# Score matmuls of a head pair as two 64-row array tiles, with the PSUM banks divided 5, 1, 2 instead of 3, 2, 3

## The chip, the cores and the metric

The kernel runs on one core of one Trainium2 chip. The metric is the device time of the kernel in microseconds (us), measured on that core. "Clock" is the share of full speed that the throttle granted TensorE. A profile is of one execution; its "span" is some 2 us shorter than the time.

## The reference

Eight batches of causal attention (by blocks of 64), eight heads of 64, sequence 576, followed by a token-mixing and a channel-mixing layer on the concatenated heads. Cut to what matters:

```python
# q, k, v: [8, 8, 576, 64] fp32, normal x 0.1
scores = q @ k.T / 8;  mask: 64-row block of the query >= 64-row block of the key
x  = softmax(scores) @ v                     # -> [8, 576, 512], heads side by side
h  = relu(x.T @ w_tok1) @ w_tok2             # token mix: 576 -> 256 -> 576
u  = x + h.T
out = u + relu(u @ w_ch1) @ w_ch2            # channel mix: 512 -> 1536 -> 512
```

## The kernel before

All matmuls are in bf16. The MLP of one batch runs between the attention of the next, and a scheduler orders the instructions of each engine. Per batch there are four head pairs. Q and K of a pair are transposed together, so head 0 lies in partitions 0 to 63 and head 1 in 64 to 127. The eight PSUM banks are divided among three pools, and every tile below takes one bank.

```python
ps_at = tile_pool("ps_at", bufs=3, PSUM)   # scores; probabilities times V also go here
ps_tr = tile_pool("ps_tr", bufs=2, PSUM)   # transposes of q, k and u
ps_mm = tile_pool("ps_mm", bufs=3, PSUM)   # MLP matmuls
...
# attention_pair: K of one head, the other head's 64 rows being zero (set at the start)
nc.vector.tensor_copy(kTh[0][0:64, :], kT_ps[0:64, :])        # L194
nc.scalar.copy(kTh[1][64:128, :], kT_ps[64:128, :])           # L195
for hh in range(2):
    kT = kTh[hh]
    sc = [ps_at.tile([128, 512], FP32, name="sc") for _ in range(4)]
    for J, (tix, c0, ist, wdt) in REGIONS.items():            # L214: 6 matmuls, 1600 columns
        nc.tensor.matmul(out=sc[tix][:, c0:c0+wdt], lhsT=kT[:, j0:j0+128],
                         rhs=qT[:, ist:ist+wdt], ...)         # 128 rows, 64 of them zero
    nc.scalar.activation(e[0], sc[0], EXP, scale=scale)       # L223 .. L226: 3 large, 1 small
    ...
    # L238: 15 matmuls of 65 columns into sc[3]; then normalised into x_sb
...
# transpose_u: for each of 5 row blocks: 4 transposes into ONE ps_tr bank (L301),
#              then nc.any.tensor_copy out of it (L306, mostly ScalarE)
# channel_gT:  24 groups of 4 matmuls of 288 columns into a ps_mm bank (L319),
#              each followed by a ReLU out of it (L326)
```

The softmax here doesn't subtract the row's maximum and nothing guards it: scores larger than these inputs give would overflow.

## Time and profile before

| | before |
|---|---|
| time, median of 2 runs | 415.43 us (415.31 to 415.54) |
| span of the profile | 412.9 us |
| TensorE recorded busy | 89% |
| ScalarE busy | 54% |
| one batch in the steady state | 46.2 us |

The waits of TensorE in the kernel before; the columns are engine, tile and line that waited, the releaser, then total us, number of waits, longest us.

```profile
PE sc L214 <- ACT e L223: 2.9, 15, 0.3
...
PE trp L301 <- ACT uT L306: 0.8, 2, 0.6
```

Scores and transposes wait for ScalarE for 3.7 us in the whole run. This is TensorE's timeline around one head pair of the kernel before (start us, length us, line, operation, count; in brackets idle time just before and its releaser):

```profile
222.89 0.82 PE L214 MATMUL sc<-qT,kTa 128*128 128x512 bf16 x5
223.55 0.59 PE L336 MATMUL mps<-wc_sb,gT 128*128 128x512 bf16 x2
224.22 0.19 PE L214 MATMUL sc<-qT,kTa 128*128 128x64 bf16 x1
224.25 0.59 PE L336 MATMUL mps<-wc_sb,gT 128*128 128x512 bf16 x2
224.71 0.38 PE L214 MATMUL sc<-qT,kTb 128*128 128x512 bf16 x1
```

Between the score matmuls (L214) stand matmuls of the second channel layer (L336).

### The profile page before, as it was taken

To read this page: it belongs to the slowest core of one execution; us is meant where nothing else is said; L and a number is where in the kernel's file an instruction comes from. 1 tells how busy PE (TensorE), PEld (TensorE's weight loads), DVE (VectorE), ACT (ScalarE), POOL (GpSimd) and SP (SyncE) were. 2 spreads that over 40 slices of the span, in tenths; PEclk is the share of its full clock that TensorE was granted. 3 is DMA by queue.
4 is the path that set the end of the run, shared out by engine and by line. 5 is a ranking of instruction groups with operands and counts; after the bars stand their busy time and mean duration, and the time that the engine had idled before them with its cause. 6 is when DMAs were issued, how large, how long until landed. Compare 5 with 4: busy or idle time off the path is not lost.

```text
span 412.9 us, 8622 instructions
## 1 busy us (share of the span) xinstructions
PE 368.6 (89%) x3194; PEld 229.3 (56%) x3232; DVE 175.8 (43%) x674; ACT 221.4 (54%) x507; POOL 261.0 (63%) x403
## 2 busy tenths in 40 slices
PE   1676659999999999999999999999999999999996
PEld 1454247754676456744666457744666457744752
DVE  2244324543545364543554363543555363534112
ACT  9635037742677058742687058732687068730830
POOL 9999389999999775983679375973679320000000
PEclk9998859999999999999999999999999999999999
DMA  6999999999988894785668494885658550003003
GB/s 40 103 60 111 206 78 58 59 60 152 74 58 57 52 156 31 51 54 128 42 41 54 33 154 30 52 52 129 44 38 51 51 110 0 2 2 114 2 2 114
DMA packets 124730, 27.91 MB, mean 68 GB/s; under 512 B 117200, under 2 KB 119568, under 8 KB 124688
## 3 DMA queue, kind: packets, MB, share of 16 engines
q0 software_dynamic: 119824, 17.92, 60.2%
q1 hardware_dynamic: 4864, 9.44, 6.3%
q8 instruction: 26, 0.43, 0.4%
q14 instruction: 16, 0.13, 0.1%
HBM read 35.78 MB, written 9.44 MB: 110 GB/s over the span
## 4 chain that ended last, share of the span: by engine, by line
PE 52%; ACT 22%; POOL 9%; DVE 8%; DMA 5%; issue 3%; ACTq 0%; POOLq 0%
PE mps L336 22%; PE mps L319 18%; ACT e L224 6%; ACT e L223 5%; ACT kTb L195 5%; DMA wc_sb<-in_moe_w_ch_dram 4%; PE sc L238 4%; ACT e L225 3%; PE sc L214 3%; DVE u_sb L290 3%; POOL qraw L116 2%; POOL v L202 2%; ACT uT L306 2%; DVE qT L188 1%; ACT gT L326 1%
## 5 line engine op out<-in xcount | busy, mean ns | idle before, releaser
L319 PE MATMUL mps<-uT,wc_sb 128*128 128x288 bf16 x768 | 111.6, 286 | 1.0
L336 PE MATMUL mps<-wc_sb,gT 128*128 128x512 bf16 x464 | 110.8, 379 | 0.8
L319 PEld LDWEIGHTS <-wc_sb 128*128 128x128 bf16 x768 | 71.0, 97 | 28.4 <-issue 10.6
L116 POOL DMA_DIRECT2D qraw<-in_q_dram x64 | 55.3, 864 | 43.8 <-PE trp L192 28.8
L326 ACT ACTIVATE gT<-mps 128x288 bf16<-128x288 f32 x144 | 59.0, 410 | 28.1 <-PE mps L319 20.7
L336 PEld LDWEIGHTS <-gT 128*128 128x128 bf16 x480 | 44.5, 98 | 50.8 <-issue 5.1
L195 ACT COPY kTb<-trp 64x640 bf16<-64x640 bf16 x32 | 22.0, 687 | 89.5 <-DVE kTa L194 89.1
L202 POOL DMA_DIRECT2D v<-in_v_dram x64 | 56.3, 880 | 21.4 <-PE sc L214 18.5
L116 POOL DMA_DIRECT2D kraw<-in_k_dram x64 | 56.5, 883 | 7.0 <-PE trp L192 5.2
L343 DVE TENSOR_TENSOR o_sb<-mps,u_sb 128x512 f32<-128x512 f32 (+1 forms) x40 | 27.6, 690 | 71.3 <-PE mps L336 71.3
L238 PEld LDWEIGHTS <-e 128*128 128x128 bf16 x960 | 41.6, 101 | 16.9 <-issue 6.9
L214 PE MATMUL sc<-qT,kTb 128*128 128x64 bf16 (+4 forms) x190 | 43.7, 292 | 2.9 <-issue 0.4
L122 POOL DMA_DIRECT2D kraw<-in_k_dram x64 | 42.3, 660 | 1.0 <-DMA wc_sb<-in_moe_w_ch_dram 1.0
L122 POOL DMA_DIRECT2D qraw<-in_q_dram x64 | 40.9, 640 | 2.7 <-DMA wc_sb<-in_moe_w_ch_dram 2.7
L238 PE MATMUL sc<-v,e 128*128 128x65 bf16 x900 | 41.7, 195 | 1.1 <-ACT e L226 0.8
L206 POOL DMA_DIRECT2D v<-in_v_dram x64 | 41.4, 647 | 0.4 <-PE sc L214 0.3
L225 ACT ACTIVATE e<-sc 128x512 bf16<-128x512 f32 x60 | 36.0, 600 | 3.3 <-PE sc L214 1.5
L224 ACT ACTIVATE e<-sc 128x512 bf16<-128x512 f32 x60 | 35.7, 595 | 3.7 <-PE sc L214 3.7
L223 ACT ACTIVATE e<-sc 128x512 bf16<-128x512 f32 x60 | 35.8, 597 | 3.4 <-PE mps L238 1.9
L306 ACT COPY uT<-trp 128x512 bf16<-128x512 bf16 (+1 forms) x36 | 19.5, 544 | 29.9 <-PE trp L301 28.8
L326 DVE TENSOR_SCALAR gT<-mps 128x288 bf16<-128x288 f32 x48 | 22.0, 458 | 26.1 <-PE mps L319 25.6
L214 PE MATMUL sc<-qT,kTa 128*128 128x64 bf16 (+4 forms) x162 | 27.8, 280 | 4.3 <-ACT e L223 2.6
(61 smaller groups left out, 367.9 us busy)
## 6 DMA issues: line engine op xcount, KB each, us to landing
out_dram<-o_sb SPq DMA_DIRECT2D x8, 1024.0 KB, 4.3
qraw<-in_q_dram POOLq DMA_DIRECT2D x64, 64.0 KB, 2.8
kraw<-in_k_dram POOLq DMA_DIRECT2D x64, 64.0 KB, 2.7
v<-in_v_dram POOLq DMA_DIRECT2D x64, 64.0 KB, 2.8
wc_sb<-in_moe_w_ch_dram POOLq DMA_DIRECT2D x4, 384.0 KB, 6.8
wc_sb<-in_moe_w_ch_dram POOLq DMA_DIRECT2D x6, 256.0 KB, 11.9
qraw<-in_q_dram POOLq DMA_DIRECT2D x64, 8.0 KB, 2.3
kraw<-in_k_dram POOLq DMA_DIRECT2D x64, 8.0 KB, 2.3
```

The costliest lines, as they stand in the source:

```text
L116: nc.gpsimd.dma_start(out=t[:, c0:c1, hh, :], in_=src[b, 2 * hp + hh, 128 * c0 : 128 * c1, :].rearrange("(c p) d -> p c d", p=128),)
L122: nc.gpsimd.dma_start(out=t[0:64, 4, hh, :], in_=src[b, 2 * hp + hh, 512:576, :])
L195: nc.scalar.copy(kTh[1][64:128, :], kT_ps[64:128, :])
L202: nc.gpsimd.dma_start(out=v1[:, 0:4, 0:64], in_=v[b, h, 0:512, :].rearrange("(c p) d -> p c d", p=128),)
L214: nc.tensor.matmul(out=sc[tix][:, c0 : c0 + wdt], lhsT=kT[:, j0 : j0 + 128], rhs=qT[:, ist : ist + wdt], start=True, stop=True,)
L223: nc.scalar.activation(e[0], sc[0], EXP, scale=scale)
L224: nc.scalar.activation(e[1][:, 0:512], sc[1], EXP, scale=scale)
L225: nc.scalar.activation(e[2][:, 0:512], sc[2], EXP, scale=scale)
L238: nc.tensor.matmul(out=u_view[:, I, 0:65], lhsT=exp_lhsT(e, I, J), rhs=v1[:, J, 0:65], start=(J == 0), stop=(J == I),)
L319: nc.tensor.matmul(out=g_ps[:, 0:288], lhsT=wc1_sb[:, m, 128 * cc : 128 * (cc + 1)], rhs=uT[:, m, 288 * sh : 288 * (sh + 1)], start=(m == ...
L326: nc.any.tensor_scalar_max(gT[:, cc, 288 * sh : 288 * (sh + 1)], g_ps[:, 0:288], 0.0)
L336: nc.tensor.matmul(out=h2_ps, lhsT=gT[:, cc, 128 * si : 128 * (si + 1)], rhs=wc2_sb[:, cc, :], start=(cc == 0), stop=(cc == NDC - 1),)
```

## The change

The intent: a score matmul contracts over 64 rows, and before it used all 128 rows of the array with zeros in half of them. Two matmuls on the two halves of the array can run side by side, so the 3200 columns of a head pair would take the time of 1600; K need not be padded, so one copy of it is enough instead of two on two engines. To have both heads' scores in flight, the score pool gets five banks; one bank is taken from the transposes and one from the MLP. Cut to its core:

```diff
-    ps_at = ... bufs=3     ps_tr = ... bufs=2     ps_mm = ... bufs=3
+    ps_at = ... bufs=5     ps_tr = ... bufs=1     ps_mm = ... bufs=2
...
-        kTh = [r_kta.next(), r_ktb.next()]
-        nc.vector.tensor_copy(kTh[0][0:64, :], kT_ps[0:64, :])
-        nc.scalar.copy(kTh[1][64:128, :], kT_ps[64:128, :])
+        kT = r_kt.next()
+        nc.vector.tensor_copy(kT[:, 0:S], kT_ps[:, 0:S])
...
+    BANKS = ((0, ((0, 0, 128, 0, 512),)),
+             (1, ((0, 0, 128, 512, 64), (64, 128, 128, 128, 448))),
+             (2, ((0, 256, 128, 256, 320), (320, 384, 128, 384, 192))),
+             (3, ((330, 512, 64, 512, 64),)))
+        for bank, regions in BANKS:
+            for hh in range(2):
+                scs[hh].append(ps_at.tile([128, 512], FP32, name="sc"))
+            for c0, j0, jn, ist, wdt in regions:
+                for hh in range(2):
+                    r = slice(64 * hh, 64 * hh + 64)
+                    nc.tensor.matmul(out=scs[hh][bank][0:jn, c0:c0 + wdt],
+                                     lhsT=kT[r, j0:j0 + jn], rhs=qT[r, ist:ist + wdt], ...)
+            for hh in range(2):
+                nc.scalar.activation(...)   # the exponential of this bank, both heads
```

The rings of e grow from 3 to 4, and the zeroing of the padded K tiles at the start goes (cut).

More of the change, by code (lines that the diff above doesn't have):

```diff
@@ L67 @@
     small_p = ctx.enter_context(tc.tile_pool(name="small_p", bufs=4))
-    ps_at = ctx.enter_context(tc.tile_pool(name="ps_at", bufs=3, space=bass.MemoryType.PSUM))
-    ps_tr = ctx.enter_context(tc.tile_pool(name="ps_tr", bufs=2, space=bass.MemoryType.PSUM))
-    ps_mm = ctx.enter_context(tc.tile_pool(name="ps_mm", bufs=3, space=bass.MemoryType.PSUM))
+    ps_at = ctx.enter_context(tc.tile_pool(name="ps_at", bufs=5, space=bass.MemoryType.PSUM))
+    ps_tr = ctx.enter_context(tc.tile_pool(name="ps_tr", bufs=1, space=bass.MemoryType.PSUM))
+    ps_mm = ctx.enter_context(tc.tile_pool(name="ps_mm", bufs=2, space=bass.MemoryType.PSUM))
     r_qraw = Ring(ring_p, 4, [128, NS, 2, D], BF16, "qraw")
     r_kraw = Ring(ring_p, 4, [128, NS, 2, D], BF16, "kraw")
-    r_kta = Ring(ring_p, 4, [128, SP], BF16, "kTa")
-    r_ktb = Ring(ring_p, 4, [128, SP], BF16, "kTb")
+    r_kt = Ring(ring_p, 4, [128, SP], BF16, "kT")
     r_v1 = Ring(ring_p, 6, [128, NS, 66], BF16, "v1")
-    r_e0 = Ring(ring_p, 3, [128, 512], BF16, "e0")
-    r_e1 = Ring(ring_p, 3, [128, 576], BF16, "e1")
-    r_e2 = Ring(ring_p, 3, [128, 576], BF16, "e2")
-    r_e3 = Ring(ring_p, 3, [128, 128], BF16, "e3")
+    r_e0 = Ring(ring_p, 4, [128, 512], BF16, "e0")
+    r_e1 = Ring(ring_p, 4, [128, 576], BF16, "e1")
+    r_e2 = Ring(ring_p, 4, [128, 576], BF16, "e2")
+    r_e3 = Ring(ring_p, 4, [128, 128], BF16, "e3")
     r_x = Ring(ring_p, 3, [128, NS, DM], BF16, "x_sb")
@@ L88, in init_pads @@
             nc.vector.memset(t[64:128, 4], 0.0)
-        for t in r_kta.tiles:
-            nc.scalar.memzero(t[64:128, :])
-        for t in r_ktb.tiles:
-            nc.scalar.memzero(t[0:64, :])
         for t in r_v1.tiles:
@@ L160, in load_channel_weights @@
             )
+    BANKS = (
+        (0, ((0, 0, 128, 0, 512),)),
+        (1, ((0, 0, 128, 512, 64), (64, 128, 128, 128, 448))),
+        (2, ((0, 256, 128, 256, 320), (320, 384, 128, 384, 192))),
+        (3, ((330, 512, 64, 512, 64),)),
+    )
     REGIONS = {
@@ L192, in attention_pair @@
             nc.tensor.transpose(kT_ps[:, 128 * c : 128 * (c + 1)], kraw[:, c], ident)
-        kTh = [r_kta.next(), r_ktb.next()]
-        nc.vector.tensor_copy(kTh[0][0:64, :], kT_ps[0:64, :])
-        nc.scalar.copy(kTh[1][64:128, :], kT_ps[64:128, :])
+        kT = r_kt.next()
+        nc.vector.tensor_copy(kT[:, 0:S], kT_ps[:, 0:S])
+        vs, scs, es = [], [[], []], []
         for hh in range(2):
             h = 2 * hp + hh
-            kT = kTh[hh]
             v1 = r_v1.next()
@@ L206, in attention_pair @@
             nc.gpsimd.dma_start(out=v1[0:64, 4, 0:64], in_=v[b, h, 512:576, :])
-            sc_pool, sc_name = (
-                (ps_mm, "mps") if (b == 0 and hh == 0) else (ps_at, "sc")
-            )
-            sc = [sc_pool.tile([128, 512], FP32, name=sc_name) for _ in range(4)]
-            for J, (tix, c0, ist, wdt) in REGIONS.items():
-                j0 = 128 * (J if J != 5 else 0)
-                nc.tensor.matmul(
-                    out=sc[tix][:, c0 : c0 + wdt],
-                    lhsT=kT[:, j0 : j0 + 128],
-                    rhs=qT[:, ist : ist + wdt],
-                    start=True,
-                    stop=True,
-                )
-            e = [r_e0.next(), r_e1.next(), r_e2.next(), r_e3.next()]
-            nc.scalar.activation(e[0], sc[0], EXP, scale=scale)
-            nc.scalar.activation(e[1][:, 0:512], sc[1], EXP, scale=scale)
-            nc.scalar.activation(e[2][:, 0:512], sc[2], EXP, scale=scale)
-            nc.scalar.activation(
-                e[3][0:64, 0:64], sc[3][0:64, 330:394], EXP, scale=scale
-            )
+            vs.append(v1)
+            es.append([r_e0.next(), r_e1.next(), r_e2.next(), r_e3.next()])
+        for bank, regions in BANKS:
[4 more added lines that the diff above has]
+                    r = slice(64 * hh, 64 * hh + 64)
+                    nc.tensor.matmul(
+                        out=scs[hh][bank][0:jn, c0 : c0 + wdt],
+                        lhsT=kT[r, j0 : j0 + jn],
+                        rhs=qT[r, ist : ist + wdt],
+                        start=True,
+                        stop=True,
+                    )
+            for hh in range(2):
+                if bank < 3:
+                    nc.scalar.activation(
+                        es[hh][bank][:, 0:512], scs[hh][bank], EXP, scale=scale
+                    )
+                else:
+                    nc.scalar.activation(
+                        es[hh][3][0:64, 0:64],
+                        scs[hh][3][0:64, 330:394],
+                        EXP,
+                        scale=scale,
+                    )
+        for hh in range(2):
+            h = 2 * hp + hh
+            e, sc, v1 = es[hh], scs[hh], vs[hh]
             nc.vector.memset(e[0][64:128, 0:64], 0.0)
```

## The prediction

> **What bounds the kernel now.** I read the busy table and the slices first.
>
> ```profile
> PE 368.6 (89%) x3194; PEld 229.3 (56%) x3232; DVE 175.8 (43%) x674; ACT 221.4 (54%) x507; POOL 261.0 (63%) x403
> ...
> PE   1676659999999999999999999999999999999996
> ...
> DMA  6999999999988894785668494885658550003003
> ```
>
> TensorE works nine tenths or more of every slice from about 62 us on. Before that the loads hold it (DMA nine tenths, TensorE one to seven); the change leaves those loads alone. So the body is TensorE's, and the question is how much of its "busy" is streaming. The groups give durations of one instruction; a duration contains the latency of the array, which neighbours overlap.
>
> ```profile
> L319 PE MATMUL mps<-uT,wc_sb 128*128 128x288 bf16 x768 | 111.6, 286 | 1.0
> L336 PE MATMUL mps<-wc_sb,gT 128*128 128x512 bf16 x464 | 110.8, 379 | 0.8
> ...
> L238 PE MATMUL sc<-v,e 128*128 128x65 bf16 x900 | 41.7, 195 | 1.1 <-ACT e L226 0.8
> ...
> L225 ACT ACTIVATE e<-sc 128x512 bf16<-128x512 f32 x60 | 36.0, 600 | 3.3 <-PE sc L214 1.5
> ...
> L306 ACT COPY uT<-trp 128x512 bf16<-128x512 bf16 (+1 forms) x36 | 19.5, 544 | 29.9 <-PE trp L301 28.8
> ```
>
> The spacing of a run is what a matmul costs. In the timeline 28 matmuls of 288 columns take 3.59 us: (3.59 - 0.286) / 27 = 0.122 us each, against a duration of 0.286. In the same way 43 of 512 columns take 9.44 us, 0.216 each; 15 of 65 columns 0.63 us, 0.031 each; 5 transposes 0.44, 0.056 each. Next the table by stretches: in the steady state one batch takes 46.2 us.
>
> ```profile
> 228.70:274.98 46.28, 44.27 (x400) 27.62 (x404) 21.99 (x82) 26.33 (x59) 31.34 (x49) 1.00 0.68 65
> 274.98:321.20 46.22, 44.26 (x399) 27.64 (x404) 21.97 (x82) 26.33 (x59) 31.09 (x49) 1.00 0.68 65
> ```
>
> Streaming one batch costs: first channel layer 96 x 0.122 = 11.8; second 60 x 0.216 = 12.9; token mix 20 x 0.216 = 4.3; transposes 60 x 0.056 = 3.3; probabilities times V 120 x 0.031 = 3.8; scores, eight heads of 1600 columns, 8 x 0.68 = 5.5. Sum 41.6 of 46.2: 4.6 us per batch are waits on TensorE. Where they are is in the timeline of one batch:
>
> ```profile
> 245.70 0.38 PE L301 MATMUL trp<-ident,u_sb 128*128 128x128 bf16 x4
> ...
> 245.96 0.59 PE L283 MATMUL mps<-aT,w_sb 128*128 128x512 bf16 x2
> ...
> 246.12 2.51 ACT L306 COPY uT<-trp 128x512 bf16<-128x512 bf16 x4 [1.77 <-PE trp L301]
> ...
> 246.39 0.39 PE L301 MATMUL trp<-ident,u_sb 128*128 128x128 bf16 x4
> ...
> 247.02 0.40 PE L301 MATMUL trp<-ident,u_sb 128*128 128x128 bf16 x4 [0.24 <-DVE u_sb L290]
> ...
> 249.30 3.59 PE L319 MATMUL mps<-uT,wc_sb 128*128 128x288 bf16 x28
> ...
> 249.98 3.35 ACT L326 ACTIVATE gT<-mps 128x288 bf16<-128x288 f32 x7 [0.74 <-PE mps L319]
> ...
> 253.97 0.60 PE L214 MATMUL sc<-qT,kTa 128*128 128x64 bf16 x4 [0.19 <-issue]
> ...
> 254.13 0.69 ACT L195 COPY kTb<-trp 64x640 bf16<-64x640 bf16 x1
> ...
> 254.84 0.60 ACT L223 ACTIVATE e<-sc 128x512 bf16<-128x512 f32 x1
> ...
> 255.33 0.59 ACT L224 ACTIVATE e<-sc 128x512 bf16<-128x512 f32 x1
> ...
> 255.49 0.19 PE L214 MATMUL sc<-qT,kTa 128*128 128x64 bf16 x1 [0.18 <-ACT e L223]
> ```
>
> L301 transposes u, L306 copies the transposes out of PSUM, L319 is the first channel layer, L214 the scores, L223 and L224 the first two exponentials of a head. I take four figures from these lines. A copy or activation starts 0.04 us after the recorded end of the matmul it needs (245.70 + 0.38, then 246.12). TensorE starts 0.05 us after the activation that frees its bank (254.84 + 0.60, then 255.49). Exponentials start 0.49 us apart though each is recorded as 0.60. With three banks the first channel layer runs at its streaming rate, seven ScalarE activations in 3.35 us: no wait at all. The u transposes, with two banks, stand 0.6 to 0.7 us apart, which is the pace of the ScalarE copy (0.585).
>
> **What the Trainium skill says.** "TensorE: Matmul & The Clock Gate", section "Back-to-back issue gap", gives N/2.4 + 2.5 ns warm: 215.8 ns for 512 columns, and the trace has 216; its Part 3, "Packing small matmuls", says that tiles in different row groups run concurrently, starting about 4 ns apart. "TensorEngine Tiling (Array Packing)", "Key Properties", says that changing the tiling mode drains TensorE; "PSUM Bottleneck" there says that tiling speeds TensorE but not the evacuation. The trace of before has only 128*128 tiles, so it can show neither concurrency nor drain.
>
> **The change, part by part.** I compared the two programs' order on each engine; TensorE runs in order, so a blocked matmul blocks all behind it.
>
> Scores. If pairs run concurrently, 1600 columns per head pair replace 3200: 0.68 us saved per pair, 2.7 per batch. But in the new order the eleven score matmuls of a pair stand together, with nothing between. Five banks are filled (bank 0, 1 of both heads, bank 2 of the first); the sixth waits for the first exponential to free one. From the first score at 0: scores end 0.38, exponential 0.42 to 1.02, so the sixth bank starts at 1.07, while the matmuls before it took 0.57. The small 64-column tile of the first head waits for the second exponential, 0.91 to 1.51, and starts at 1.56. So 0.5 + 0.3 = 0.8 us of waiting comes in for the 0.68 saved. Even if the two tiles did not overlap, the end of this clump would be 1.56: its pace is ScalarE's.
>
> ScalarE and VectorE. The 32 copies of K by ScalarE (0.687 us each, 22 us) go; exponentials of a pair start 0.42 instead of 0.87 us after the first score. VectorE copies K once, at about its former 0.47. ScalarE's long wait before it, 89 us in 16 waits for VectorE's half of the copy, goes too, but ScalarE is busy only 26.3 of 46.2 us and waits for TensorE, so little of it is on the path. The zeroing of the padded K tiles at the start (eight of about 0.45 us) goes as well, and lies under the loads.
>
> One transpose bank. Each u transpose group must wait for the copy of the one before: 3 x 0.056 + 0.219 + 0.04 + 0.585 + 0.05 = 1.06 us per group, where two banks gave about 0.65. The new order puts almost nothing between: from the first group to the second matmul group of the channel layer I get 4 x 1.06 + 0.85 = 5.1 us (0.85 for the last, half-size copy), holding 2.0 us of work. Before, the same stretch took 3.6 us with 2.3 us of work. Loss 1.8 us per batch.
>
> Two MLP banks. A bank's loop in the first channel layer is 0.49 (four matmuls) + 0.21 (latency of the last) + 0.41 (ScalarE) + 0.05 = 1.16 us for two groups, against 2 x 0.49 = 0.98 streaming: 0.09 us lost per group where groups stand in a row, as eight do after the u transposes (0.7 us), and 24 in the last batch (2.1 us). In the second layer a group lasts 2.6 us and an evacuation 0.69, so nothing is lost. In the token mix the second VectorE result comes late: its matmul pair waits about 0.75 us, and a later one 0.4.
>
> I then walked one steady batch in the new order with these figures, from the first score of a pair to that of the next: pair 1 to 2: 7.65 us (before 7.52); 2 to 3: 7.6 (7.63); 3 to the next batch's 0, second layer between: 16.7 (16.87); 0 to 1, with token mix, u transposes and eight groups in a row: 16.7 (14.21). Together +2.4 us per batch with drains free. The clump costs as much as it saves; the loss is in the last stretch.
>
> Drains. The order changes tiling five times per pair: into 64x128, to 64x64 (the last, narrow tile), back to 128x128, again 64x64, back. What a drain costs I estimate from the trace: a 65-column matmul is recorded as 0.19 us and costs 0.03 in a run, so an emptied array loses about 0.16. The first two fall partly or wholly into waits (K copy, second exponential). Three by 0.16 remain, less about 0.15 taken up by later waits that exist anyway (the last exponential before V): 0.3 us per pair, guessed between 0.1 and 0.6.
>
> Sum. Full steady batches from the second batch's pair 1 to the last's: 6 x 2.4 = 14.6. Start of the second batch, partly under loads: 1.2. Last batch without attention: transposes 2.4 and groups in a row 2.1 = 4.5. Drains 28 pairs x 0.3 = 8.4. First batch (loads): 0. 415.4 + 28.7 = 444.1 us.
>
> **Rivals.** (1) The tiles win: scores are 5.5 us of each batch and half goes, 8 x 2.7 = 22 us, 394 us or less. For it: TensorE is the bound. Against: freed time is only worth something if the next instruction is ready, and the new order gives the clump nothing else to do than wait for the exponentials. (2) The waits were there already: 4.6 us per batch on TensorE; if the new waits only replace these, the time stays near 415. Against: before, score matmuls are spread between channel-layer groups that fill such waits, and the transposes have two banks. (3) Drains are dear (0.3 us with the weight load, none hidden): 28 x 1.2 = 34 us on top of 436, 470 us. (4) Tiles do not overlap: no difference to 444, since the clump ends with the exponentials.
>
> **Range and chances.** Drains at 0.1 to 0.6 us per pair give 438 to 452; the walk may be off by 1 us per batch either way. 80% range 430 to 456. It takes an error of 20 us in the walk to come under 424, hence slower 0.91, within 2% 0.06, faster 0.03.
>
> **What would show it.** Steady batch near 49.8 us. Waits of score matmuls for exponentials grow from about 3 us to 15 or more in total; of transposes for the ScalarE copy from about 1 us to over 15; of the channel layer for its own activation from nothing to 5 or more. Pairs of score matmuls start within some ns of each other. The last 24 groups take about 14 us instead of 12. The prediction is wrong if the clump takes much less than 1.5 us, if the u transposes stay near 0.6 us apart, or if a switch of tiling costs nothing or far more than 0.2 us.

## The result, and the profile after

The changed kernel took 439.79 us (median of two runs, 439.23 and 440.35), against 415.43 of before. The ratio is 1.059, with a 95% interval from 1.055 to 1.064. Here and below a ratio is the mean time of one kernel's runs over that of the other's runs of the same rounds, so it is not quite the ratio of the medians quoted. The result lies in the predicted range, 4.3 us under the predicted point.

The span grew by 24.6 us (412.9 to 437.5). I cut it at the first score matmul of the second head pair, in the second batch (68.95 us before, 72.82 after) and in the last one (346.21 and 367.13; the record of the matmul at 346.21 is missing, so this is the time of its weight load):

| stretch | before | after | more |
|---|---|---|---|
| start, to the second batch | 68.95 | 72.82 | 3.9 |
| six steady batches | 6 x 46.21 | 6 x 49.05 | 17.0 |
| last batch and its MLP, to the end | 66.69 | 70.37 | 3.7 |

The steady batch again in the table by stretches, of the kernel after (columns as in the prediction's table: us, then busy us and instructions of TensorE, its weight loads, VectorE, ScalarE, GpSimd; clock; DMA share; GB/s):

```profile
269.03:318.08 49.05, 44.50 (x401) 25.97 (x405) 21.41 (x81) 23.49 (x57) 31.30 (x49) 1.00 0.65 62
```

Then the busy table of the page of after and its costliest group, which answers to L319 before:

```profile
PE 373.4 (85%) x3202; PEld 215.9 (49%) x3232; DVE 172.0 (39%) x666; ACT 195.8 (45%) x478; POOL 259.9 (59%) x403
...
L328 PE MATMUL mps<-uT,wc_sb 128*128 128x288 bf16 x768 | 119.4, 286 | 4.1 <-ACT uT L315 3.7
```

TensorE's recorded busy time rose by 4.8 us although 21.6 us of score columns (32 pairs by 0.675) now run beside others; ScalarE's fell by 25.6 us. The group L328 has the same 768 matmuls as before, the same mean duration, and yet 119.4 instead of 111.6 us of busy time. The idle time before it rose by 3.1 us. A matmul of 288 columns has a recorded duration of 0.286 us but costs 0.122 in a stream, so a wait of up to 0.16 us lies under the recorded duration of the matmul before it and shows as no idle time. About 5 of the 7.8 us can be seen to be such waits: 0.51 us in each run of 28 matmuls (below), and 1.9 us in the run of 92 in the last batch (13.29 us; 11.43 in e3 below, which has three MLP banks). The rest I did not trace.

The waits of TensorE, after:

```profile
PE trp L310 <- ACT uT L315: 12.0, 27, 0.7
PE sc L216 <- ACT e L225: 9.6, 30, 0.3
```

And where they are. This is the timeline of one pair's score block, all engines, with lines left out:

```profile
318.08 0.74 PE L216 MATMUL sc<-qT,kT 64*128 64x512 bf16 x7
318.50 3.05 ACT L225 ACTIVATE e<-sc 128x512 bf16<-128x512 f32 x6 [0.16 <-PE sc L216]
...
319.15 0.67 PE L216 MATMUL sc<-qT,kT 64*128 64x320 bf16 x4 [0.33 <-ACT e L225]
...
319.76 0.66 PE L328 MATMUL mps<-uT,wc_sb 128*128 128x288 bf16 x4
...
320.35 0.21 PE L216 MATMUL sc<-qT,kT 64*64 64x64 bf16 x1
...
320.50 0.42 PE L328 MATMUL mps<-uT,wc_sb 128*128 128x288 bf16 x2
```

The eleven score matmuls of the block now stand together, and the sixth bank waits: first score 318.08, first exponential at 318.50 (0.42 later), its end 319.1, sixth bank at 319.15 (1.07). The channel layer, which stands behind the scores in TensorE's order, resumes at 319.76, 1.68 us after the first score, and the narrow tile of the second head starts at 320.35. The last of the four matmuls from 319.15 on is the narrow tile of the first head; counted back from their end, it starts at 319.64 (1.56). The first seven matmuls really overlap: in windows of 0.01 us the first two start together at 318.08, and six are in flight from 318.34 to 318.46. In e5 below, where the two heads share one half of the array, the second starts about 0.2 us after the first, and at most four are in flight. So the pairing works, and its gain is spent waiting.

Last, TensorE's timeline at the transposes of u in the same batch, after:

```profile
309.17 0.38 PE L310 MATMUL trp<-ident,u_sb 128*128 128x128 bf16 x4 [0.21 <-ACT uT L315]
310.23 0.38 PE L310 MATMUL trp<-ident,u_sb 128*128 128x128 bf16 x4 [0.67 <-ACT uT L315]
...
311.29 0.38 PE L310 MATMUL trp<-ident,u_sb 128*128 128x128 bf16 x4 [0.18 <-ACT uT L315]
312.13 4.10 PE L328 MATMUL mps<-uT,wc_sb 128*128 128x288 bf16 x28 [0.46 <-ACT uT L315]
```

With one bank the transposes start 1.06 us apart, the time of a full round: transpose, ScalarE copy, next transpose. The 28 matmuls of the channel layer take 4.10 us where they took 3.59 with three banks.

### The profile page after: what moved, and what is told of

Read it like the earlier page. It is cut to its first block, busy times and chain, and to the rows that moved or that the text cites. A ratio compares the mean times of both kernels' runs of the same rounds, so it can differ in the third digit from the quotient of the medians.

```text
span 437.5 us, 8593 instructions
## 1 busy us (share of the span) xinstructions
PE 373.4 (85%) x3202; PEld 215.9 (49%) x3232; DVE 172.0 (39%) x666; ACT 195.8 (45%) x478; POOL 259.9 (59%) x403
## 4 chain that ended last, share of the span: by engine, by line
PE 74%; ACT 9%; POOL 6%; DMA 6%; issue 2%; DVE 2%; ACTq 0%; POOLq 0%
PE mps L345 24%; PE mps L328 24%; PE sc L216 6%; PE sc L247 6%; ACT uT L315 4%; ACT e L225 4%; PE mps L275 4%; PE trp L310 3%; PE mps L292 3%; DMA wc_sb<-in_moe_w_ch_dram 2%; PE trp L194 2%; DMA qraw<-in_q_dram 2%; PE trp L188 2%; POOL qraw L111 1%; DMA w_sb<-in_moe_w_tok_dram 1%
## 5 line engine op out<-in xcount | busy, mean ns | idle before, releaser
L328 PE MATMUL mps<-uT,wc_sb 128*128 128x288 bf16 x768 | 119.4, 286 | 4.1 <-ACT uT L315 3.7
L225 ACT ACTIVATE e<-sc 128x512 bf16<-128x512 f32 x192 | 97.6, 615 | 50.7 <-PE sc L216 50.7
L345 PE MATMUL mps<-wc_sb,gT 128*128 128x512 bf16 x464 | 107.6, 379 | 0.8
L328 PEld LDWEIGHTS <-wc_sb 128*128 128x128 bf16 x768 | 69.0, 97 | 30.2 <-issue 16.5
L216 PE MATMUL sc<-qT,kT 64*128 64x320 bf16 (+5 forms) x384 | 53.0, 298 | 15.4 <-ACT e L225 9.6
L216 PEld LDWEIGHTS <-kT 64*128 64x128 bf16 (+1 forms) x384 | 17.9, 99 | 57.4 <-issue 41.2
L283 ACT ACTIVATE aT<-mps 128x512 bf16<-128x512 f32 x8 | 4.8, 597 | 91.7 <-PE mps L275 91.7
L247 PEld LDWEIGHTS <-e 128*128 128x128 bf16 x960 | 38.1, 103 | 8.8 <-issue 4.2
L190 DVE COPY qT<-trp 128x640 bf16<-128x640 bf16 x32 | 15.6, 488 | 62.3 <-PE trp L188 62.2
L188 PE MATMUL trp<-ident,qraw 128*128 128x128 bf16 x160 | 20.3, 232 | 13.3 <-DMA qraw<-in_q_dram 13.3
L299 DVE TENSOR_TENSOR u_sb<-mps,x_sb 128x512 bf16<-128x512 f32 (+1 forms) x40 | 26.6, 683 | 3.3 <-PE mps L292 2.4
```

The costliest lines, as they stand in the source:

```text
L188: nc.tensor.transpose(qT_ps[:, 128 * c : 128 * (c + 1)], qraw[:, c], ident)
L216: nc.tensor.matmul(out=scs[hh][bank][0:jn, c0 : c0 + wdt], lhsT=kT[r, j0 : j0 + jn], rhs=qT[r, ist : ist + wdt], start=True, stop=True,)
L225: nc.scalar.activation(es[hh][bank][:, 0:512], scs[hh][bank], EXP, scale=scale)
L247: nc.tensor.matmul(out=u_view[:, I, 0:65], lhsT=exp_lhsT(e, I, J), rhs=v1[:, J, 0:65], start=(J == 0), stop=(J == I),)
L328: nc.tensor.matmul(out=g_ps[:, 0:288], lhsT=wc1_sb[:, m, 128 * cc : 128 * (cc + 1)], rhs=uT[:, m, 288 * sh : 288 * (sh + 1)], start=(m == ...
L345: nc.tensor.matmul(out=h2_ps, lhsT=gT[:, cc, 128 * si : 128 * (si + 1)], rhs=wc2_sb[:, cc, :], start=(cc == 0), stop=(cc == NDC - 1),)
```

## The experiments

The kernel before was run in the same rounds: its medians were 414.93 (e1 to e4), 414.84 (e5 to e7), 414.87 (e8 to e11) and 414.58 us (e12). "Wrong on purpose" means that the scores computed are not the reference's; e5, e6 and e8 nevertheless passed the comparison of outputs. The inputs have a deviation of 0.1, so scores are small and softmax is nearly uniform; that this is why they passed is an inference. Agreement of the output therefore says little about the scores.

The theory after the result: the loss is the banks (one for the transposes, two for the MLP, and the score block that five banks let the scheduler put together, paced by the exponentials) plus the tiling changes. The rivals: the tiles themselves are slow or do not overlap; or drains are most of it.

**e1: the bank split alone, without tiles**

```diff
 # kernel before
-ps_at 3, ps_tr 2, ps_mm 3
+ps_at 5, ps_tr 1, ps_mm 2
-    (ps_mm, "mps") if (b == 0 and hh == 0) else (ps_at, "sc")
+    (ps_at, "sc")
```

> The kernel before (zero-padded K, full-array scores, ScalarE K copy) with the new bank split 5 score, 1 transpose, 2 MLP. If the bank split is the loss, as the prediction has it (u transposes 1.8 us and channel layer 0.7 us per batch, 4.5 us in the last batch), it takes about 437 us (433 to 442) with u transpose groups 1.06 us apart. If the 64-row tiles and their drains are the loss, the split alone costs little and it stays under 421 us.

434.39 us, ratio 1.047 [1.045, 1.048]: 19.5 us slower with no tile in it. A steady batch took 48.34 us (one of them 1.3 us more, with a fall of the clock as in e3). In batch 0 the scores of each pair's first head, which the kernel before puts into ps_mm, go to ps_at here, as in the kernel after. Of the 24.4 us lost, the split alone makes the greater part.

**e2, e3, e4: the kernel after with other splits**

```diff
 # kernel after: ps_at, ps_tr, ps_mm
-5, 1, 2
+4, 2, 2      # e2
+4, 1, 3      # e3
+3, 2, 3      # e4, the split of before
```

> The changed kernel with 4 score, 2 transpose, 2 MLP banks. Bank theory: the u transposes come back to 0.6 to 0.7 us apart, 1.8 us per batch for 7 batches and 2.4 in the last, about 15 us off: 425 us (420 to 431). The score matmuls are then split up into more pieces (eleven changes of tiling per pair in place of five), which at about 0.11 us each could give back up to 0.66 us per pair. Rival, drains dominate: as slow as the changed kernel or slower, 440 us or more.

432.67 us, 1.043 [1.041, 1.045]. The transposes' loss came back (TensorE's waits there for the ScalarE copy fell from 12.0 to 3.3 us), but I had expected 425. The pairs cost more: 8.01 us from one pair to the next instead of 7.76. With four score banks the block waits 0.46 us for an exponential after its sixth matmul and then is spread among the channel layer; in the trace that makes eight to ten changes of tiling per pair (I had expected eleven) instead of five. The result lies between my range (420 to 431) and the rival's (440 or more).

> The changed kernel with 4 score, 1 transpose, 3 MLP banks. Bank theory: only the rows of channel-layer groups recover, 0.7 us per batch and 2.1 us in the last, about 7 us off: 433 us (428 to 437); transposes still 1.06 us apart. Rival as before: 440 us or more.

445.81 us, 1.075 [1.074, 1.077], the slowest of all; I had expected 433, and this is in the range set for the rival (changes of tiling dominate, 440 or more). So the bank theory as I had it is not enough for e2 and e3: with four score banks the order changes too. The third MLP bank did what it should (28 matmuls in 3.59 us again), but the pairs cost 8.0 us as in e2. In addition four of the six steady batches lost another 1.1 to 1.4 us. This is the table by stretches of e3, two successive steady batches:

```profile
195.32:246.37 51.05, 46.32 (x400) 26.79 (x404) 21.32 (x82) 23.50 (x56) 31.52 (x49) 0.97 0.62 59
246.37:296.07 49.70, 44.97 (x401) 26.12 (x405) 21.33 (x82) 23.50 (x56) 31.55 (x49) 1.00 0.63 61
```

and in the first of the two, the stretch of the u transposes and one of the microseconds at half clock:

```profile
213.00:216.00 3.00, 1.26 (x14) 0.79 (x12) 2.35 (x6) 1.52 (x3) 1.57 (x3) 1.00 0.78 49
...
218.00:219.00 1.00, 0.67 (x3) 0.41 (x3) 0.00 (x0) 0.28 (x1) 0.00 (x0) 0.50 0.00 0
```

Clock is the third column from the right. After transposes that stand 1.06 us apart, the first four with nothing between, TensorE was granted half its clock for some 3.5 us, from the last transposes to the middle of the channel run. The instructions of the second batch are the same, at the same spacing, and the clock did not fall; the kernel after has the same spacing of transposes, with a few more matmuls between, and its six steady batches all took 49.05 us. So this costs about 1.3 us in some batches, and I did not foresee it; what decides whether it comes is not shown.

> The changed kernel with the old split 3 score, 2 transpose, 3 MLP banks: the tiles alone. Bank theory: all of the split's loss comes back; what is left is 0.2 us per pair of streaming saved (only the first bank's matmuls still stand as a pair), against about twelve changes of tiling per pair at 0.11 us: 423 us (416 to 430). If tile drains were the main loss it would be 435 us or more; if the tiles are a gain that the split hid, under 410 us.

428.48 us, 1.033 [1.031, 1.034], in range. With the split of before the tiles are still 13.6 us slower than the padded kernel, though transposes and MLP have their banks back and TensorE waits only 2.8 us for exponentials. In the order of the program one sees why: three banks are filled by the first head's bank 0, the second's bank 0 and the first's bank 1, and after that the scores come head by head, one bank at a time, among matmuls of the channel layer. So most of the pairs no longer stand side by side, and there are some twelve changes of tiling per pair.

**e5, e6, e7: what the concurrency and the tiles are worth, with 5, 1, 2**

```diff
 # kernel after
-                    r = slice(64 * hh, 64 * hh + 64)
+                    r = slice(0, 64)     # e5: both heads on the same rows, one after the other; wrong on purpose
+                    r = slice(0, 128)    # e6: all rows, no tiles; wrong on purpose
-        (3, ((330, 512, 64, 512, 64),)),            # narrow tile, 64 of K's columns
+        (3, ((330, 512, 128, 512, 64),)),           # e6 and e7: 128 columns
-        nc.vector.tensor_copy(kT[:, 0:S], kT_ps[:, 0:S])
+        nc.vector.tensor_copy(kT, kT_ps)            # e6 and e7
```

> The changed kernel, but both heads of a pair use array rows 0 to 63, so that no two score matmuls can run side by side; order, banks and tilings are unchanged. Wrong result on purpose (head 1 repeats head 0's scores). Theory: the block of scores is paced by the exponentials that free its banks, so taking the concurrency away costs at most 0.1 us per pair: within 4 us of the changed kernel (437 to 444 us), although 0.68 us of streaming per pair comes back. Rival: the concurrency is a real gain that the bank split hides; then 28 x 0.68 = 19 us slower, about 459 us.

440.31 us, 1.062 [1.059, 1.064], against 439.79 of after. With the concurrency removed nothing changes; a steady batch takes 49.06 us, against 49.05. The same block in e5's timeline of TensorE:

```profile
317.96 1.75 PE L216 MATMUL sc<-qT,kT 64*128 64x512 bf16 x11
319.64 0.66 PE L328 MATMUL mps<-uT,wc_sb 128*128 128x288 bf16 x4
```

The channel layer resumes at 319.64: 1.68 us after the first score, in both kernels. But concurrency does show where TensorE itself is the pace. The first block of the second batch runs at half clock in both (TensorE had waited some 5 us for loads), and there the same eleven matmuls took (after, then e5):

```profile
58.15 2.06 PE L216 MATMUL sc<-qT,kT 64*128 64x512 bf16 x11 [0.55 <-DVE kT L196]
```

```profile
57.47 2.92 PE L216 MATMUL sc<-qT,kT 64*128 64x512 bf16 x11 [0.55 <-DVE kT L196]
```

So two tiles side by side save 0.86 us of a block of 2.92 us. At full clock the saving lies under the exponentials.

> The changed kernel, but each score matmul contracts all 128 rows of the unpadded K and Q and the last K block is 128 wide: one tiling throughout, no concurrency, same banks and nearly the same order. Wrong result on purpose (the two heads' scores are added). Against e5 it differs by the drains alone. Theory: three exposed changes per pair at about 0.11 us, partly absorbed: 0.1 to 0.35 us per pair, 3 to 9 us below e5. Rival, drains free: same time as e5; drains dear (0.3 us each, none hidden): 25 us or more below.

435.50 us, 1.050 [1.047, 1.052]. The difference between e5 and e6 is the tiling alone, with no concurrency in either: 4.8 us, 0.17 us per pair over 28 pairs. In the steady state, where the clock is full in both, it is 49.06 less 48.42 per batch, 0.16 per pair; outside it the two profiles differ by chance of the clock too (e5 was at half clock for some 3.5 us in its last batch, and e6 was granted full speed later in the second).

> The changed kernel with the last K block 128 wide, so that the narrow 64x64 tiling goes and the number of changes of tiling per pair falls from five to four (the one that goes lies in the wait for the second exponential). Right result. Theory: no measurable gain, within 2 us of the changed kernel. Rival: if the 64x64 tiling is itself slow, 5 us or more faster.

439.22 us, 1.059 [1.056, 1.062]: no effect, as expected. The 64-column tile is not a cost of its own.

**e8, e9, e10, e11: no tiles, and the split of before**

```diff
 # e8: e6 with ps_at, ps_tr, ps_mm = 3, 2, 3 (wrong on purpose)
 # e9: as e8, but right: Q of each head is padded with zero rows (zeroed once at the start), K is copied once, unpadded
+        qT = [r_qta.next(), r_qtb.next()]
+        nc.vector.tensor_copy(qT[0][0:64, :], qT_ps[0:64, :])
+        nc.scalar.copy(qT[1][64:128, :], qT_ps[64:128, :])     # e10: nc.vector.tensor_copy
-                        lhsT=kT[r, j0 : j0 + jn], rhs=qT[r, ist : ist + wdt],
+                        lhsT=kT[:, j0 : j0 + jn], rhs=qT[hh][:, ist : ist + wdt],
 # e11: the kernel before, head after head, with Q padded in this way instead of K
```

> e4 (old split 3, 2, 3) with every score matmul over all 128 rows of the unpadded K and Q, nearly the same order: the same score matmuls without tilings. Wrong result on purpose (the two heads' scores are added). In the trace of e4 four score columns groups and two channel-layer matmuls take 0.67 us per round where they stream in 0.46: 0.10 us per change of tiling, about twelve per head pair. If those drains are what keeps e4 behind the kernel before, this one wins 1.0 us per pair less what waits absorb: 413 us (405 to 420). Rival: e4's loss lies in the interleaved order of the two heads; then it stays at 425 us or more.

405.29 us, 0.977 [0.976, 0.979]. Against e4 only the tiles are gone (and the narrow K tile, which e7 shows to be free): 23.2 us, 0.83 us per pair. In the steady state it is 47.94 less 44.91 us per batch, 0.76 per pair; 2.9 us more lie before the second pair of the second batch, where e4 also had half clock for longer. Where the time of a change lies can be read by comparing one round, two score matmuls of one head and two of the channel layer. First e4, then e8, TensorE's timeline (the channel matmuls between, L328, are the lines left out):

```profile
273.01 0.39 PE L216 MATMUL sc<-qT,kT 64*128 64x320 bf16 x2
...
273.68 0.39 PE L216 MATMUL sc<-qT,kT 64*128 64x320 bf16 x2
```

```profile
249.73 0.38 PE L216 MATMUL sc<-qT,kT 128*128 128x320 bf16 x2
...
250.22 0.38 PE L216 MATMUL sc<-qT,kT 128*128 128x320 bf16 x2
```

The columns to be streamed are the same. A round takes 0.67 us with tiles (273.01 to 273.68) and 0.49 without (249.73 to 250.22). That is 0.18 us for two changes of tiling, 0.09 us each. It is a lower bound: e8's exponentials start 0.49 us apart without a pause here, so its round is at ScalarE's pace; the columns alone would take 0.46 (two by 0.122 and 512 by 0.216 / 512), which gives 0.10 per change (an estimate from these numbers). The first round of a pair takes 1.07 us in both kernels, since the next score waits for the first exponential, so neither the pair of 512 columns that stands side by side in e4 nor the changes there count. From the first score to V it is 4.34 us (271.28 to 275.62) against 3.59 (248.17 to 251.76), and these 0.75 us are the 0.76 of the steady state.

> A right version of e8: Q instead of K is zero-padded per head (VectorE copies one half, ScalarE the other), K is copied once and is full width; split 3, 2, 3, heads interleaved bank by bank. If e8 is right about the drains: 415 us (408 to 421), level with the kernel before or a little under it. If the ScalarE copy of Q gets into the way of the exponentials: 422 us or more.

408.26 us, 0.985 [0.983, 0.986], with the reference's scores. This version beats both kernels: 6.6 us under before, 1.5%, well outside the interval. A steady batch takes 45.26 us. Of the change it keeps the order of the scores, bank by bank for both heads, and the single K copy; it drops tiles and split.

> e9 with both halves of Q copied by VectorE. ScalarE is freed of 22 us, but K's copy stands 0.48 us later behind the second Q copy. Expected within 4 us of e9; ScalarE theory: faster than e9; critical K copy theory: slower.

409.59 us, 0.987 [0.986, 0.989]: both halves of Q by VectorE is a little slower than sharing with ScalarE.

> The kernel before, one head after the other as it was, but with Q padded instead of K, so that the ScalarE copy is of Q, earlier, and no longer stands between the K transposes and the first exponential. Expected 412 us (406 to 417): at most 0.45 us per pair, 28 x 0.45 = 13 us, if that wait is exposed; nothing if channel-layer groups fill it.

412.24 us, 0.994 [0.993, 0.996]. Padding Q instead of K in the old order gives 2.6 us; the other 4.0 us of e9 come with the new order of the scores (and the fourth buffer of e, which was not tested alone).

**e12: shorter exponentials**

```diff
 # kernel after, wrong on purpose; e is set to a constant at the start
-                        es[hh][bank][:, 0:512], scs[hh][bank], EXP, scale=scale
+                        es[hh][bank][:, 0:256], scs[hh][bank][:, 0:256], EXP, scale=scale
```

> The kernel after, but each large exponential handles only the first 256 of the 512 columns of its bank (the rest of e is a constant set at the start); wrong on purpose. Scores, tiles and banks are those of the kernel after; in TensorE's program order the two narrow 64x64 tiles now stand together at the end of the block, which takes away two tiling changes per pair. Theory (the exponentials pace the block): a large exponential shrinks from 0.60 to about 0.39 us (256 columns fewer at the 0.82 ns per column that 0.42 us for 512 columns gives, an estimate), so the sixth score bank starts about 0.86 us after the first score instead of 1.07, and the block ends near 1.5 us instead of 1.68 although it holds one more matmul; time 426 to 434 us, of which about 5 us (28 pairs by two changes of 0.09 us) belong to the tiling changes. Rival (the tiles, or their changes, pace the block): the sixth bank stays at 1.07 us, and the time is 434 to 438, the two changes alone.

431.51 us, 1.040 [1.039, 1.042]; the output is wrong, as it must be. The large exponentials took 0.391 us. TensorE's timeline of one block:

```profile
311.51 1.59 PE L216 MATMUL sc<-qT,kT 64*128 64x512 bf16 x12
313.04 0.91 PE L328 MATMUL mps<-uT,wc_sb 128*128 128x288 bf16 x6
```

In narrow windows the sixth bank's score is seen to start at 312.37, 0.86 us after the first, and the channel layer resumes at 313.04, 1.53 us after the first score though one matmul more stands before it. From one pair to the next it was 7.39 us instead of 7.76. The exponential, not the array, sets when the sixth bank starts. Of the 8.3 us gained I had put about 5 down to the two tiling changes fewer per pair, and the scheduler also moved some channel groups behind V; the run shows what sets the sixth bank and the end of the block, not how the gain divides.

The four kernels with the scores interleaved by bank make a square:

| | split 3, 2, 3 | split 5, 1, 2 | the split costs |
|---|---|---|---|
| full rows (e8, e6) | 405.3 | 435.5 | 30.2 |
| tiles (e4, after) | 428.5 | 439.8 | 11.3 |
| the tiles cost | 23.2 | 4.3 | |

The two costs do not add. With three banks the scheduler spreads the scores, so nothing waits for an exponential but the tiling changes twelve times; with five it puts them in one block, which changes five times and waits. The left column pays for changes, the right one for waits.

## Why the prediction was right, and where it was off

**The sign and the mechanism: right.** The prediction said that the score block is paced by ScalarE and that freed TensorE time would not reach the end. Its times within the block were 0.42 (first exponential), 1.07 (sixth bank) and 1.56 (the first narrow tile); measured 0.42, 1.07 and 1.56, with the channel layer 0.12 later. e12 moved the second of them to 0.86 by shortening the exponentials, with the order up to there unchanged, and e5 took the concurrency away at no cost. Rival 1 (the tiles win 22 us) and rival 2 (the waits were there already) are out; rival 4 (tiles do not overlap) is out as a fact, and right in that it makes no difference. Rival 3 (drains at 1.2 us per pair; five changes by its 0.3 would even be 1.5) is wrong for this order and nearer for e4's, 0.76.

Two of its readings of the trace of before were wrong, without harm to the sum. The first exponential is not 0.87 us after a pair's first score: there the record of the first score matmul is missing, its weight load starts at 253.74, and the distance is 1.1 (0.69 in the pair at 222.89). And the u transposes, 0.6 to 0.7 us apart, were not at the pace of the ScalarE copy: the line shown has "DVE u_sb" as the releaser, and of their waits before 2.6 us were for VectorE's u and 0.8 for the copy.

**One transpose bank: right.** 1.06 us per group was predicted and measured, and 5.1 us from the first group to the channel run (307.06 to 312.13, 5.07).

**Two MLP banks: right in kind, a little large.** Predicted 1.16 us for two groups, 0.09 lost per group; measured 4.10 for seven groups against 3.59, 0.07 per group. In the last batch 23 groups took 13.12 us, 0.57 each against 0.50 before.

**The walk through a steady batch: near.** With its drains (0.3 per pair) the four stretches were 7.95, 7.9, 17.0 and 17.0; measured 7.76, 7.78, 16.92 and 16.59. The batch came out at 49.05 instead of 49.8.

**Term by term**, with drains at 0.16 us per pair (e5 less e6 in the steady state). The prediction's terms add to the time, the measured ones to the span:

| term of the sum | predicted | measured |
|---|---|---|
| six batches, without drains | 14.6 | 13.3 (17.05 less 24 x 0.158) |
| drains, 28 pairs | 8.4 | 4.4 |
| start of the second batch, without its drain | 1.2 | 3.7 |
| last batch, without its drains | 4.5 | 3.2 |
| sum | 28.7 | 24.6 |

The drains were the largest mis-sized term. The step was "Three by 0.16 remain, less about 0.15": a change cost 0.09 to 0.10 us, not 0.16, where e4 and e8 let it be seen. Five of them are some 0.5 us per pair; 0.16 of it reaches the time, the rest lies presumably in the waits, as the step assumed for two of the five.

The start was under-sized, and partly hid the error of the drains: that the total came so near is in part luck. The step took the start as one batch's share "partly under loads". Of its 3.7 us, 0.4 are there before the second batch's first transposes, which wait for a load (55.23 us before, 55.63 after; 54.95 in e5). One part of the reason is the bank: with a single one the u transposes stand behind the K transposes and the whole score block and begin at 60.13 us, where before they began at 56.63. The other part is the clock, which the step did not think of. The table by stretches in this place, first of before, then of after:

```profile
64.00:65.00 1.00, 1.00 (x21) 0.87 (x20) 0.23 (x2) 0.33 (x2) 1.00 (x3) 1.00 0.87 56
```

```profile
64.00:65.00 1.00, 1.00 (x16) 0.97 (x14) 0.88 (x5) 0.00 (x0) 1.00 (x3) 0.50 0.56 35
```

The third column from the right is the clock. Before was granted full speed again from 62.4 us on; after, whose TensorE waited more, only from 66.8 (that the waits are the cause is not shown). Some 4.4 us more at half speed are up to 2.2 us of lost streaming (an estimate from these two times), and 3.7 less 2.2 is near the 1.2 of the prediction. Most of the other kernels agree: e2, e4 and e6 were granted full speed at about 67 us or later and began the second pair's scores at 71.87, 71.50 and 73.52; e8 was granted it at 62 and began them at 68.64, earlier than before. e5 fits less well: granted it at 65.6, it began them at 72.69.

**The signs in the profile: half right.** The score waits for exponentials were to be 15 us or more, and the profile has 9.6; transposes 15, it has 12.0; the channel layer's waits for its own activation 5, and it has no such line at all. (That paired scores start within some ns is seen only to the 0.01 us above.) The losses are there (the timelines above), but they are counted as waits only beyond the recorded duration of the matmul before. In each block the sixth bank waits 0.50 us (1.07 less 0.57), of which 0.33 are recorded; 30 times 0.50 would have been the 15 us. I had worked out the waits from the pace and then expected to find them whole in a view that shows only the part that exceeds the latency. For the channel layer the missing part is in the group's busy time.

What stays open: how e12's gain divides between exponentials and changes, the exact division of the start, and why e3's clock fell in four equal batches of six.

## What to carry to other kernels

Before pairing small matmuls on an array, ask what the next instruction waits for: here the freed time was handed to the exponentials, and the same pairing was worth 0.86 us per block where the array was the pace and nothing where it was not. A bank taken from a loop that alternates between two engines cost the whole latency of that loop here (1.06 us per transpose group), and a tiling change cost about 0.1 us each time, so count both per block in the program's order and not in the source. When the parts of a change are separable, run the square: here the best version (1.5% faster than before) used a part that nobody had meant as the gain, the order of the scores with a single unpadded K.

## What the Trainium skill lacked or had wrong

- "TensorEngine Tiling (Array Packing)", "Key Properties", says that changing the tiling mode drains TensorE, and gives no size. Here one change cost 0.09 to 0.10 us (a round of 0.67 us with two changes in it, against 0.49 measured without and 0.46 of columns), 23.2 us over the kernel when the scores were spread (e4 against e8, some of it the clock). Its "PSUM Bottleneck" (tiling speeds up TensorE and not the evacuation of PSUM) holds: six matmuls were in flight at once, and taking the pairing away moved the time only from 439.79 to 440.31 us.
- "TensorE: Matmul & The Clock Gate", Part 1, has an idle window as the cause of the fall to half clock in its table of states, and "A second HAM failure mode" adds frequent short idle times between groups of matmuls; neither says how thin is too thin. In e3 the fall (clock 0.50, some 3.5 us long, about 1.3 us lost) came after a stretch in which TensorE was recorded busy for 1.26 of 3.00 us, with a transpose group every 1.06 us; and it came in four of six batches with the same instructions.
- "Perfetto Trace Analysis", "Identifying the Most-Contended Engine", calls matmul busy time a poor measure: TensorE's busy time rose by 4.8 us while its work fell. The page doesn't say that a wait shorter than the array's latency is recorded inside the matmul before it: here one group's lost time shows as 7.8 us more "busy", about 5 of which can be traced to such waits, and 3.1 more "idle".
- No page has a check that the order of the program keeps paired tiles side by side; with three score banks the scheduler put them head by head, and the tiled kernel took 428.48 us against 405.29 without tiles.
